# GpSimd's constants written during the decay, rows on ScalarE's queue, second weights right behind the first: one change to an attention-and-MoE kernel

## The chip, the cores and the metric

The kernel runs on one core of a Trainium2 chip. The metric is device time in microseconds (us) of one execution; a kernel is run several times and its median is given with the lowest and the highest run. Profiles come from one execution each, and their span is some 2 us shorter than the time of the run. PE is the matmul engine TensorE, PEld its weight loads, DVE is VectorE, ACT is ScalarE, POOL is GpSimd, SP is SyncE, and a "q" behind a name (SPq, ACTq) is the part of that engine that issues DMAs.

## The reference, cut to what matters

```python
# attention with a decay: q, k, v are (8, 8, 576, 64), f is (8, 8, 576)
scores = scale * np.matmul(q, k.transpose(0, 1, 3, 2))
cum = np.cumsum(np.log(np.clip(f, 0.0001, 1.0)), axis=-1)
scores = np.where(causal, -1e9, scores + cum[:, :, :, None] - cum[:, :, None, :])
attn = softmax(scores)                      # written out in the reference
x = (attn @ v) as (8, 576, 512)
# moe: w_in (512, 1024), a 3-tap convolution along the sequence, w_out (1024, 512)
h = np.maximum(x @ w_in, 0.0)               # "moe1" in this text
conv_out = sum(conv_w[k] * shifted(h, k) for k in range(3))
out = (h * sigmoid(conv_out)) @ w_out       # "moe2"
```

## The kernel before

Heads are worked four at a time: a **half batch** is four heads of one batch, and there are sixteen; two heads are a **pair**. Q and K of a half batch are loaded transposed by SP into a ring of buffers, and the decay enters the scores as extra rows of these buffers: high and low parts of the cumulative sums (`khi`, `klo`), written by small DMAs. VectorE "clamps" those buffers (it turns some rows into constants), the scores are multiplied, ScalarE takes the exponentials, the product with V is normalised ("norm", VectorE), transposed, and when both half batches of a batch are through, moe1 of that batch starts.

The head of the kernel is written out by hand. The rest is a list of tasks with estimated times; a function plays them through once, with a model of each engine and of the DMA traffic, and every engine's instructions are then written in the order in which the play started them. The engines keep that order on the chip, whatever they find there. I call this function **the planner**.

```python
def rows_first(p, eng):                       # the decay's rows of half batch 0
    eng.dma_start(tq[126:127, c], khi4[r, :])
    eng.dma_start(tk[96:97, c], khi4[r, :])
    eng.dma_start(tk[98:99, c], klo4[r, :])
# ... the head, in this order: decay of the first four heads, rows_first(0, nc.scalar),
# decay of all heads, then
rows_first(1, nc.gpsimd)
load_v(0, 0, HH); load_v(0, HH, H)
nc.gpsimd.dma_start(kd[0], khi_sb)            # the decay's copies in DRAM
nc.gpsimd.dma_start(kd[1], klo_sb)
# ... then GpSimd's constants: ones and zeros in va, ident, borders of ht
# ... tasks; keys are priorities, the lowest goes first
WAITS = ((3, 0), (3, 1), (4, 0), (4, 1))      # second weights behind these clamps
for j, (h, side) in enumerate(WAITS):
    if h == hb:
        x = task({"DVE": 0.1}, [even[1] if side == 0 else even[-1]], -9,
                 lambda j=j: hold(w_out_f16[:, 2 * j:2 * j + 2, :]))
        t_wout.append(task({"POOL": 0.8}, [x], 2 * hb - 1.0, lambda j=j: load_w_out(j),
                           lag=2.0, dma=1.7))
```

`hold` is a write of one element by VectorE into the weights' buffer, so that the load behind it can't start earlier.

## Time and profile before

| | before |
|---|---|
| median of 3 runs | 272.54 us (272.22 to 273.33) |
| profiled span, mean PE clock | 271.1 us, 0.976 of full |
| PE, DVE, ACT busy | 241.7, 226.9, 212.1 us |
| PE full (over 9.5 of 10 us) | from about 74 to 235 us |
| PE's holes between 44 and 72 us | 5.1 us |
| first moe1 starts | 38.33 us |

How to read it: PE is the bound for most of the run, so the time is set by how soon PE gets full and stays full. The lines that show this stand in the prediction.

### The profile page before, as it was taken

What the parts mean: (1) busy time and instruction counts of PE and PEld (TensorE: products, weight loads), DVE (VectorE), ACT (ScalarE), POOL (GpSimd) and SP (SyncE); (2) the same over time, 40 slices, a digit from 0 to 9 for tenths busy, and PEclk for the clock granted to TensorE, in tenths of its full rate; (3) what the DMA queues carried; (4) which work ended last, traced back from release to release, by engine and by line L of the source; (5) the groups of instructions that cost most, each with busy time, mean ns of one, the idle gap of its engine ahead of it and who ended that gap; (6) DMA issues with size and microseconds to landing.
All of it is one profiled execution on the core that took longest, in us unless ns stands there. A gap on an engine that the chain in (4) does not pass through costs nothing.

```text
span 271.1 us, 6621 instructions
## 1 busy us (share of the span) xinstructions
PE 241.7 (89%) x2602; PEld 166.1 (61%) x2602; DVE 226.9 (84%) x401; ACT 212.1 (78%) x347; POOL 59.2 (22%) x124
## 2 busy tenths in 40 slices
PE   2864869878899999999999999999999999989990
PEld 1333646646677777776776677667776777655540
DVE  5863538999799999999989989999899999978751
ACT  5081727989879999989989899989889998577552
POOL 4491110631120340332315050406010100000000
PEclk9999868999999999999999999999999999999997
DMA  8999999999998999999999999999101201022015
GB/s 138 202 209 177 223 184 221 222 183 246 168 220 183 219 244 166 228 167 256 269 213 180 203 245 185 223 160 278 61 28 52 80 0 58 23 116 80 0 46 226
DMA packets 121284, 44.58 MB, mean 164 GB/s; under 512 B 115560, under 2 KB 116596, under 8 KB 121254
## 3 DMA queue, kind: packets, MB, share of 16 engines
q1 hardware_dynamic: 115088, 32.00, 66.9%
q0 software_dynamic: 5840, 12.01, 17.0%
q8 instruction: 20, 0.33, 0.5%
q10 hardware_dynamic: 326, 0.17, 0.4%
q14 instruction: 10, 0.08, 0.1%
HBM read 13.99 MB, written 9.58 MB: 87 GB/s over the span
## 4 chain that ended last, share of the span: by engine, by line
PE 64%; DVE 8%; DMA 7%; issue 6%; SPq 6%; ACT 5%; POOL 0%; DVEq 0%; ACTq 0%; POOLq 0%
PE mm L425 19%; PE mm L487 19%; PE sc L298 10%; PE O L356 8%; DMA stk<-in_k_dram 6%; SPq L110 5%; PE sc L330 4%; DVE u L457 2%; PE sc L500 2%; PE mm L393 2%; DVE u L455 2%; SPq L163 1%; ACT ht L438 1%; DMA out_dram<-ob 1%; ACT po L324 1%
## 5 line engine op out<-in xcount | busy, mean ns | idle before, releaser
L425 PE MATMUL mm<-xt,w_in_f 128*128 128x288 f16 x512 | 80.3, 292 | 1.7 <-DVE xt L413 0.4
L298 PE MATMUL sc<-stq,stk 128*128 128x128 bf16 (+3 forms) x576 | 67.3, 242 | 8.1 <-ACT pm L338 3.6
L324 ACT ACTIVATE po<-sc 128x1024 f16<-128x1024 f32 x64 | 64.6, 1028 | 2.6 <-PE sc L298 2.1
L438 ACT ACTIVATE ht<-mm 128x288 f16<-128x288 f32 x128 | 52.0, 414 | 12.3 <-PE mm L425 11.2
L298 PEld LDWEIGHTS <-stk 128*128 128x128 bf16 x576 | 42.4, 99 | 28.7 <-issue 7.7
L425 PEld LDWEIGHTS <-w_in_f 128*128 128x128 f16 x512 | 48.2, 100 | 18.7 <-issue 3.1
L487 PE MATMUL mm<-w_out_f,hg 128*128 128x512 f16 x248 | 58.4, 379 | 0.7 <-ACT xt L411 0.6
L455 DVE SCALAR_TENSOR_TENSOR u<-ht,cwt 128x576 f32<-128x576 f16 x64 | 51.5, 810 | 5.4 <-ACT ht L438 4.7
L457 DVE SCALAR_TENSOR_TENSOR u<-ht,cwt,u 128x576 f32<-128x576 f16 x64 | 51.5, 810 | 0.5
L475 DVE SCALAR_TENSOR_TENSOR hg<-hg,ht 128x576 f16<-128x576 f16 x56 | 41.6, 751 | 4.4 <-ACT hg L467 4.0
L467 ACT ACTIVATE hg<-u,cwt 128x576 f16<-128x576 f32 x56 | 43.4, 780 | 1.0 <-DVE u L457 0.9
L338 ACT ACTIVATE pm<-sc 128x1024 f16<-128x1024 f32 x32 | 32.9, 1028 | 11.8 <-PE sc L298 11.7
L487 PEld LDWEIGHTS <-hg 128*128 128x128 f16 x248 | 23.5, 98 | 24.2 <-issue 0.9
L356 PE MATMUL O<-va,po 128*128 128x65 f16 x640 | 36.6, 194 | 1.2 <-ACT po L324 1.0
L356 PE MATMUL O<-va,pm 128*128 128x65 f16 x256 | 31.1, 194 | 3.0 <-DVE xn L369 1.8
L356 PEld LDWEIGHTS <-po 128*128 128x128 f16 x640 | 30.5, 97 | 2.4 <-ACT po L324 1.8
L356 PEld LDWEIGHTS <-pm 128*128 128x128 f16 x256 | 24.1, 98 | 5.7 <-DVE xn L369 2.7
L369 DVE TENSOR_TENSOR xn<-O,rc 128x640 f16<-128x640 f32 x32 | 26.4, 824 | 1.1
L132 POOL DMA_DIRECT2D stq<-consts x23 | 12.2, 535 | 66.8 <-PE mm L425 27.0
L330 PE MATMUL sc<-trib,identb 128*128 128x512 bf16 x64 | 24.5, 383 | 1.2 <-ACT po L324 1.1
L511 ACT ACTIVATE ob<-mm 128x512 f32<-128x512 f32 x23 | 13.7, 598 | 11.0 <-PE mm L487 10.7
L522 POOL DMA_DIRECT2D out_dram<-ob x10 | 7.7, 768 | 44.2 <-ACT ht L438 21.9
(112 smaller groups left out, 223.8 us busy)
## 6 DMA issues: line engine op xcount, KB each, us to landing
vf<-in_v_dram SPq DMA_DIRECT2D x64, 128.0 KB, 4.0
out_dram<-ob POOLq DMA_DIRECT2D x10, 512.0 KB, 6.4
out_dram<-ob SPq DMA_DIRECT2D x10, 256.0 KB, 2.1
stq<-consts POOLq DMA_DIRECT2D x8, 216.0 KB, 4.7
vf<-in_v_dram SPq DMA_DIRECT2D x16, 64.0 KB, 5.2
w_in_f<-in_moe_w_in_dram POOLq DMA_DIRECT2D x1, 1024.0 KB, 10.7
w_out_f<-in_moe_w_out_dram POOLq DMA_DIRECT2D x4, 256.0 KB, 5.6
out_dram<-ob SPq DMA_DIRECT2D x2, 512.0 KB, 2.8
```

Source lines behind the costliest of these rows:

```text
L298: nc.tensor.matmul(sc, stk_t[hb % RING][:, k0:k0 + 128], stq_t[hb % RING][:, q0:q0 + w], start=start, stop=stop, skip_group_check=True)
L324: nc.scalar.activation(p_of[i, s][:, 0:1024], sc_of.pop((i, s)), AF.Exp, scale=SCALE)
L330: nc.tensor.matmul(sc[:, 512 * s:512 * (s + 1)], identb, trib, start=True, stop=False, skip_group_check=True)
L338: nc.scalar.activation(p_of[i, 2], sc_of.pop((i, 2)), AF.Exp, scale=SCALE)
L356: nc.tensor.matmul(O[:, s, 65 * Q:65 * (Q + 1)], w, va[:, h, m, :], start=(m == 0), stop=(m == Q))
L425: nc.tensor.matmul(ps[:, 0:w], w_in_f16[:, cc, 128 * ff:128 * (ff + 1)], xt[:, cc, w * t:w * (t + 1)], start=(cc == 0), stop=(cc == NCC - 1))
L438: nc.scalar.activation(ht[:, 0, HT_0 + w * t:HT_0 + w * (t + 1)], ps[:, 0:w], AF.Relu)
L455: nc.vector.scalar_tensor_tensor(u, hl, cwt[:, ff, 0:1], hc, op0=ALU.mult, op1=ALU.add)
L457: nc.vector.scalar_tensor_tensor(u, hr, cwt[:, ff, 1:2], u, op0=ALU.mult, op1=ALU.add)
L467: nc.scalar.activation(hv, u, AF.Tanh, scale=cwt[:, ff, 2:3])
L475: nc.vector.scalar_tensor_tensor(hv, hv, 1.0, hc, op0=ALU.add, op1=ALU.mult)
L487: nc.tensor.matmul(ps, chunk(g, ff, c), w_out_f16[:, ff, :], start=(ff == 0), stop=(ff == NFF - 1))
```

## The change

The intent has four parts. GpSimd writes its constants while VectorE prepares the decay, and the second set of rows of half batch 0 is issued by ScalarE, so GpSimd is free for the rows of half batch 1. The copies of the decay to DRAM go behind those rows. The second weights are loaded in one go behind norm 3, right after the first weights and ahead of most of half batch 3. The planner gets other priorities (`AHEAD`: it may run attention four steps ahead instead of three). It also gets three changed estimates of times, which the cut below leaves out. `CLAMPS` and `HALVES` say from which half batch on VectorE no longer clamps Q's buffer and V is loaded in whole batches.

```diff
-    def rows_first(p, eng):
+    def rows_first(p):
-        eng.dma_start(tq[126:127, c], khi4[r, :])
+        nc.scalar.dma_start(tq[126:127, c], khi4[r, :])     # and the two others
 ...  (the loops that write GpSimd's constants move up, ahead of load_qk(1, 0, 4))
-    rows_first(1, nc.gpsimd)
+    rows_first(1)
-    nc.gpsimd.dma_start(kd[0], khi_sb)                      # now a task behind the rows of half batch 1
-    nc.gpsimd.dma_start(kd[1], klo_sb)
-    CLAMPS, HALVES, LANDING = 8, 16, 3.0
+    CLAMPS, HALVES, LANDING = 6, 8, 3.0
-    WAITS = ((3, 0), (3, 1), (4, 0), (4, 1))
+    WAITS = ((3, 2), (3, 2), (3, 2), (3, 2))                # 2: behind norm 3
 ...  (rows of half batch 1 as two tasks, one for Q's row and one for K's)
-    ... 2 * hb - 1.1 + 0.5 * p, ... cast_v
+    ... 2 * hb - 0.6 + 0.5 * p, ... cast_v
-    t_norm[i] = task({"DVE": 1.05}, [t_pv[i, 1]], i - 0.0, ...
+    t_norm[i] = task({"DVE": 1.05}, [t_pv[i, 1]], i - 1.0, ...
 ...  (relu, conv, gate and evac: keys moved likewise)
-    AHEAD, QUEUED = 3.0, 8.0
+    AHEAD, QUEUED = 4.0, 8.0
```

## The prediction

> **What bounds the kernel now.** I read the stretches of four microseconds first, because the shares of the whole span (PE 89%, DVE 84%, ACT 78%) mix stages. The columns are: stretch, its length, busy time of PE, PEld, DVE, ACT and POOL, then the granted PE clock, the DMA share and GB/s.
>
> ```profile
> 20.00:24.00 4.00, 1.24 (x31) 1.04 (x31) 1.05 (x3) 0.00 (x0) 1.45 (x3) 1.00 1.31 134
> 24.00:28.00 4.00, 2.93 (x27) 2.39 (x28) 1.91 (x5) 1.97 (x3) 0.00 (x0) 0.75 1.15 237
> 32.00:36.00 4.00, 1.94 (x43) 1.40 (x39) 2.75 (x7) 1.72 (x2) 0.38 (x1) 1.00 1.25 242
> 36.00:40.00 4.00, 2.60 (x16) 1.73 (x17) 1.22 (x3) 1.43 (x2) 0.64 (x2) 0.53 1.13 154
> 40.00:44.00 4.00, 4.00 (x24) 2.65 (x23) 2.92 (x6) 1.88 (x5) 0.50 (x1) 0.62 1.13 245
> 56.00:60.00 4.00, 2.84 (x27) 1.95 (x27) 4.00 (x9) 3.52 (x8) 0.73 (x1) 1.00 1.27 188
> ```
>
> There are three stages. Up to about 41 us every compute engine has holes while the DMA share stays above 1. From 44 to 72 us DVE is full (4.00 of 4) and PE is not: its busy times there leave 0.3+0.0+1.2+1.2+0.8+0.8+0.8 = 5.1 us. From about 74 to 235 us PE is full; the stretches of twenty microseconds there show 19.6 to 20.0. So nothing in the last stage can shorten the kernel, and what counts is how early PE gets full. PE's holes between 20 and 44 us sum to 2.8+1.1+0.0+2.1+1.4+0.0 = 7.3 us, and two cold stretches come on top (clock 0.75, then 0.53 and 0.62): the 24 moe1 matmuls from 38.33 us take 5.42 us, where eight in the full-clock stage take 0.98 us (24 would take 2.9), a loss of 2.5 us.
>
> Next, the GpSimd timeline and PE's waits, for the thing that the change names.
>
> ```profile
> 10.80 0.70 POOL L125 DMA_DIRECT2D stq<-khi  x1 [6.81 <-DVE stq L119]
> ...
> 13.64 0.31 POOL L262 MEMSET va<- 64x260 f16 x1
> ...
> 18.75 0.92 POOL L140 DMA_DIRECT2D stk<-khi_sb  x1
> ...
> 20.15 0.50 POOL L142 DMA_DIRECT2D stq<-khi_sb  x1
> ```
>
> ```profile
> PE sc L298 <- DMA stq<-khi_sb: 2.7, 1, 2.7
> ```
>
> GpSimd stands idle for 6.81 us before 10.80, then writes constants from 13.64 to 17.57, and only then issues the decay rows of half batch 1, the last of which lands at 25.07, where PE has waited 2.7 us for it.
>
> Last, the chain that ended last, which starts in the loads. Columns: start, length, what.
>
> ```profile
> 10.43 5.89 DMA stk<-in_k_dram
> 16.34 0.73 SPq L163
> ...
> 20.13 4.19 SPq L110
> 24.36 10.71 DMA stk<-in_k_dram
> 35.10 0.88 DVE stk L119
> 36.14 0.84 DVE xn L369
> 37.02 0.61 PE mm L393 x4
> 38.33 5.42 PE mm L425 x24
> ```
>
> The reader is to see that the wait of 2.7 us is not on it. The chain goes through the SP queue: K of half batch 1 lands at 16.3, the rest of V is issued, then Q and K of half batch 2; K lands at 35.1 after 10.7 us beside the first weights. Its clamp on DVE (L119) stands ahead of the norm of pair 3 (L369), although PE had that pair's product ready at 34.9. That norm gates the transpose and the first moe1.
>
> **What the Trainium skill says.** "SBUF — State Buffer", section "Who interferes with whom": GpSimd shares a port pair with VectorE, held for a whole instruction by whichever starts first, in VectorE's two-port modes or against reads of GpSimd. So constants beside VectorE's decay work could slow one of the two. In the trace of before the same memsets ran beside VectorE's 1.02 us memsets of consts, at 0.31 us each; no clash is visible, but the mixture is not the same. "DMA: Bandwidth & Descriptors", section "Latency and other measured facts", gives a longer time to the first byte for GpSimd's DMAs than for those of a hardware queue (about 1 us against 600 ns). The trace agrees in direction: the first rows took 3.2 and 3.6 us from the ACT queue, the second ones 3.8 to 4.0 us from GpSimd. The same page, section "Issuing engines are not separate DMA queues": moving an issue saves the sequencer's time only, the 16 engines are shared. "TensorE: Matmul & The Clock Gate", section "What's actually happening": after an idle window of about 3.4 us PE runs at half clock. The granted 0.53 after the holes at 32 to 38 us agrees.
>
> **The change part by part.**
>
> 1. *Constants earlier.* 13.64 to 17.64 is 4.0 us of GpSimd; they fit in the hole of 6.8 us (3.99 to 10.80). GpSimd then has only DMA issues left. Cost on the path: none, if the port does not bite.
>
> 2. *Rows of half batch 0, second part, on ACT's queue.* Three issues of about 0.55 us from 10.5, the last from 11.6; plus 3.2 us it lands at 14.8, where before PE got it at 15.96. ACT issues until 12.2 and its first exponential starts at 12.92, so ACT loses nothing. Local gain about 1 us, of which V's landing (18.2) hides most.
>
> 3. *Rows of half batch 1.* Q's row can go when Q has landed (15.4), K's rows when K has (16.3). Two rows of K at about 0.55 us and two fills at 0.55 us put the last issue near 17 to 17.5; with the 4.9 us that these rows took, the scores can start at 21.9 instead of 25.07. Local gain 3.2 us, and the cold stretch after the hole (26 to 29 us, half clock) should vanish.
>
> 4. *The decay's copies to DRAM later.* Two of 72 KB leave 12.5 to 13.6 us, where they took 17% of the engines for 3 us, 0.5 us. K of half batch 1 and V come that much sooner, and with them the SP chain: about 0.5 us.
>
> 5. *But parts 2 and 3 meet the chain.* The planner at the end of the kernel writes each engine's order once. Walking it by hand with the new constants, it still assumes K of half batch 2 before norm 3 is ready, so the clamp stays ahead of that norm on DVE. K's landing moves only by part 4, from 35.1 to about 34.6. The 3.2 us are then spent waiting there: moe1 starts about 0.5 us earlier, and again cold. On the path: -0.5 us.
>
> 6. *Second weights behind the first.* Four issues of 0.73 us and 1 MB, moved from 49-60 us to about 34-40 us. It frees GpSimd from waiting on its holds (10.0 us of waits between 36 and 60), but Q, K and V of half batch 3 get some 5 us of traffic ahead of them (first weights: 10.7 us to landing while sharing). Before, K of half batch 3 landed at 43.2 and was clamped only at 50.5, so there are 7 us of room. Second weights were first used at 76.8, which waited for the last gate of batch 0 (68.6), not for weights. On the path: 0.
>
> 7. *Priorities.* Attention may run 4 instead of 3 steps ahead, norms come earlier, gates later. One step of attention is about 2.8 us of PE by the full-clock rows and about 2.5 us of DVE; one unit of moe1 is 0.98 us of PE for 2.4 us of DVE (two of 0.81 and one of 0.75). More attention in the stage where DVE is full puts more PE work against the same DVE work, so part of the 5.1 us fills. I choose 2 us: -2.0 us.
>
> 8. *Two half batches fewer clamped on DVE.* Two clamps of 0.87 us, 1.7 us of DVE, at about 80 to 100 us where PE is full: 0. V in whole batches from batch 4 on: 0.
>
> Sum: -0.5 - 2.0 = -2.5 us. I add -0.6 us for one chance in seven that norm 3 gets ahead of that clamp and moe1 starts some 4 to 5 us sooner. 272.5 - 3.1 = 269.4 us.
>
> **The rivals.**
>
> (a) *The head's gain comes through whole.* Norm 3 is not held, PE goes from half batch 1 into moe1 at 33 us without a cold clock. For it: the first weights land near 31.6, and PE's holes and cold loss of 20 to 44 us (7.3 + 2.5 + about 1.5) are large enough. Against: the chain shows K's landing, not the rows. It would give -5 to -7 us for the head, with part 7 about 264 to 266 us.
>
> (b) *All is swallowed.* K of half batch 2 holds norm 3, priorities give nothing since ACT is at 3.5 to 3.8 of 4 in the middle stage as well. It would give 272 us.
>
> (c) *The second weights delay half batch 3 and VectorE stalls in order on its clamp.* For it: the DMA share is above 1 there and the queue's holes are short. Against: 7 us of room. It would cost 1 to 3 us, 272 to 274 us with the rest.
>
> (d) *GpSimd's constants slow VectorE's decay.* The cumulative sums and clamps (0.18 to 1.34 us each) would slip by at most one GpSimd instruction each, 0.1 to 0.9 us; the first scores, now at 12.06, would come up to 1 us later.
>
> **Range and chances.** Between (a) at 265 and (b) at 272, with the middle at 269.4, I set 266.6 to 271.9. Faster by over 2% needs less than 267.1 us, which takes (a) or a far larger part 7: 0.2. Slower by over 2% needs (c) and (d) far beyond their sizes: 0.02. The rest, 0.78, is within 2%.
>
> **What would show it.** Part 1 and 3: GpSimd's constants end before 9 us, the rows of half batch 1 are issued by 18 us, the first scores of that half batch start near 22 us and the clock stays at 1.0 until 30 us. Part 5: the chain still has K of half batch 2 landing near 34.6, its clamp, then norm 3; moe1 starts near 37.8 with a clock near 0.5. Part 7: PE's holes from 44 to 72 us shrink from 5.1 to about 3 us. If moe1 starts before 35 us, step 5 is wrong and (a) holds. If a clamp of half batch 3 waits for a DMA on DVE, (c) holds. If the first scores start after 12.6 us, (d) holds.

## The result, and the profile after

| | before | after |
|---|---|---|
| median | 272.5 us (272.22 to 273.33, 4 runs) | 276.58 us (276.01 to 277.23, 4 runs) |
| ratio | 1 | 1.0145, interval 1.0111 to 1.0179 |
| profiled span, mean PE clock | 271.1 us, 0.976 | 275.5 us, 0.954 |
| PE's holes between 44 and 72 us | 5.1 us | 6.0 us |
| first moe1 starts | 38.33 us | 40.52 us |

The change made the kernel some 4 us slower; predicted were 3.1 us in the other direction. Ratios, here and below, are the mean time of one kernel's fast runs over that of the other's from the same rounds, so they aren't quite the ratio of the medians. "Fast" leaves out runs that the records mark as slow, over 1.5% above the fastest of the same kernel.

The stretches of four microseconds after the change, columns as in the prediction (stretch, length, PE, PEld, DVE, ACT, POOL, PE clock, DMA share, GB/s):

```profile
20.00:24.00 4.00, 3.31 (x21) 1.79 (x20) 0.02 (x1) 2.14 (x4) 0.00 (x0) 0.50 1.14 229
24.00:28.00 4.00, 2.57 (x48) 1.97 (x47) 1.42 (x5) 2.71 (x3) 0.05 (x1) 0.87 1.01 199
32.00:36.00 4.00, 3.55 (x56) 2.68 (x55) 2.47 (x11) 3.15 (x4) 0.00 (x0) 1.00 1.11 192
36.00:40.00 4.00, 2.14 (x42) 1.75 (x42) 1.94 (x7) 0.83 (x2) 0.54 (x1) 0.83 1.28 190
40.00:44.00 4.00, 3.62 (x18) 2.34 (x16) 1.14 (x3) 2.09 (x4) 3.39 (x6) 0.50 1.24 178
64.00:68.00 4.00, 2.06 (x40) 1.47 (x37) 3.96 (x7) 4.00 (x6) 0.78 (x1) 1.00 1.21 147
68.00:72.00 4.00, 2.05 (x28) 1.54 (x29) 3.97 (x10) 1.01 (x2) 2.49 (x4) 0.68 1.00 204
72.00:76.00 4.00, 4.00 (x22) 2.54 (x21) 3.60 (x6) 2.15 (x6) 0.00 (x0) 0.50 1.24 199
```

The same three last stretches of the kernel before:

```profile
64.00:68.00 4.00, 3.23 (x53) 2.30 (x52) 3.93 (x7) 3.58 (x6) 0.00 (x0) 1.00 1.30 244
68.00:72.00 4.00, 3.18 (x47) 2.54 (x47) 3.54 (x5) 3.22 (x5) 1.23 (x2) 1.00 1.01 200
72.00:76.00 4.00, 3.93 (x59) 3.14 (x57) 2.46 (x4) 3.91 (x8) 0.79 (x2) 1.00 1.15 166
```

Two things are new. In the head the clock is at 0.50 from 20 to 24 us, where before it was at 1.00. And from 64 to 72 us PE has only 2.06 and 2.05 us of work, after which its clock falls to 0.50: the 22 matmuls from 72 to 76 us, in part of other shapes, fill the same four microseconds as 59 did before. Up to 72 us PE had done 66 matmuls of moe1 and 144 of the scores, before 70 and 172. From 80 us on PE is full in both kernels, so the 4 us were lost before that.

First the head. GpSimd (start, length, then what ended the idle time before):

```profile
4.03 0.51 POOL L238 MEMSET va<- 64x260 f16 x1
...
7.21 0.11 POOL L245 MEMSET ht<- 128x4 f16 x1
...
15.32 1.10 POOL L141 DMA_DIRECT2D stk<-khi_sb  x1 [0.28 <-DMA stk<-in_k_dram]
```

The constants lie where they were meant to lie, and the rows of half batch 1 are issued at 15.32 where before it was 18.75. ScalarE, in the same profile:

```profile
18.14 0.47 ACTq L127 DMA_DIRECT2D stk<-klo  x1
18.66 1.02 ACT L338 ACTIVATE pm<-sc 128x1024 f16<-128x1024 f32 x1 [12.36 <-DMA stk<-khi]
```

ScalarE stands idle for 12.36 us before its first exponential at 18.66, which came at 12.92 before. It's held by its own three row DMAs, issued at 15.12, 16.19 and 18.14, where GpSimd had issued them at 10.80, 11.49 and 12.03 before. The waits in the compiled program say why (this list is not from the profile):

```
ACT: L125 rows of stq  waits DMAHW0 and DVE     owner so far: K of half batch 1 (SP)
ACT: L126 rows of stk  waits DMAHW3 and DVE     owner so far: V, first DMA (SP)
ACT: L127 rows of stk  waits DMAHW6             owner so far: V, third DMA (SP)
```

All DMAs of SP and ACT share eight completion semaphores, DMAHW0 to DMAHW7, handed out in turn by the framework that builds the program. The row DMAs got those of K of half batch 1 and of two loads of V, and each first waits until that load has landed. The trace bears this out: by its semaphore records the three loads landed at 15.04, 16.11 and 18.12, and the three issues follow within 0.1 us of them. On GpSimd's queue the same DMAs waited for VectorE alone.

Next the chain that ended last (start, length, what):

```profile
22.71 4.87 DMA stk<-in_k_dram
...
35.09 0.78 DVE stk L119
...
36.03 0.83 DVE xn L369
...
38.32 0.82 DVE xn L369
...
40.52 4.00 PE mm L425 x16
```

The clamp of half batch 2's keys (L119) stands on DVE ahead of norm 2 (L369) now; before it stood ahead of norm 3 only. But here it took its 0.8 us and waited for no load: K of half batch 2 had landed at 27.6. The first weights, which wait for norm 0 and so for ScalarE, were issued only then:

```profile
27.95 0.86 POOL L640 DMA_DIRECT2D w_in_f<-in_moe_w_in_dram  x1 [9.12 <-DVE w_in_f L153]
```

Before, they were issued at 21.41, K loaded beside them and landed at 35.1. So ScalarE's stall makes the norms late and, by the way, K early. moe1 starts 2.2 us later and at half clock: 16 matmuls take 4.00 us (before, too, it was cold: 24 in 5.42), where eight take 0.98 us at full clock.

Last the middle. The second weights are issued early, as intended, and PE's own line (start, length) of the hole reads:

```profile
39.46 2.89 POOL L157 DMA_DIRECT2D w_out_f<-in_moe_w_out_dram  x4 [8.61 <-DVE w_out_f L153]
```

```profile
70.41 0.61 PE L393 MATMUL mm<-ident,xn 128*128 128x128 f16 x4 [1.45 <-DVE xn L369]
...
71.72 4.00 PE L425 MATMUL mm<-xt,w_in_f 128*128 128x288 f16 x16 [0.38 <-DVE xt L413]
```

PE waits for the last norms of batch 1, transposes, waits again and goes into moe1 cold. It has nothing else to do there, because of the order that the planner wrote. PE's order around that point in the three kernels that matter (tasks with their count of matmuls; from the compiled programs, not the profile):

```
before           transposes 8+4, value product 15, scores of half batch 4 ..., moe1 8
                 (the first scores of half batch 4 stand ahead of the transposes)
after            transposes 8+4, moe1 16, and only then the scores of half batch 4
after, second    scores of half batch 4, transposes 8+4, scores of half batch 4, ..., moe1 8
weights as before
```

### The profile page after: what moved, and what is told of

The parts are those of the page before. It is cut to its first block, busy times and chain, and to the rows that moved or that the text cites. A ratio compares the mean times of both kernels' runs of the same rounds, so it can differ in the third digit from the quotient of the medians.

```text
span 275.5 us, 6580 instructions
## 1 busy us (share of the span) xinstructions
PE 243.4 (88%) x2602; PEld 167.4 (61%) x2602; DVE 227.5 (83%) x404; ACT 209.6 (76%) x342; POOL 60.7 (22%) x123
## 4 chain that ended last, share of the span: by engine, by line
PE 72%; DVE 8%; ACT 7%; SPq 6%; DMA 3%; issue 2%; ACTq 0%; DVEq 0%
PE mm L425 21%; PE mm L487 19%; PE sc L298 12%; PE O L356 9%; SPq L110 5%; PE sc L330 4%; ACT po L324 2%; PE sc L500 2%; PE mm L393 2%; DMA stk<-in_k_dram 2%; DVE xn L369 1%; DMA vf<-in_v_dram 1%; ACT ht L438 1%; DVE u L455 1%; DVE hg L475 1%
## 5 line engine op out<-in xcount | busy, mean ns | idle before, releaser
L425 PE MATMUL mm<-xt,w_in_f 128*128 128x288 f16 x512 | 81.3, 296 | 2.5 <-DVE xt L413 0.8
L298 PE MATMUL sc<-stq,stk 128*128 128x128 bf16 (+3 forms) x576 | 68.3, 245 | 9.5 <-ACT pm L338 6.0
L324 ACT ACTIVATE po<-sc 128x1024 f16<-128x1024 f32 x64 | 65.3, 1028 | 2.1 <-PE sc L298 1.5
L298 PEld LDWEIGHTS <-stk 128*128 128x128 bf16 x576 | 43.2, 100 | 31.3 <-issue 11.3
L425 PEld LDWEIGHTS <-w_in_f 128*128 128x128 f16 x512 | 48.8, 100 | 19.4 <-issue 4.0
L438 ACT ACTIVATE ht<-mm 128x288 f16<-128x288 f32 x128 | 51.1, 413 | 11.1 <-PE mm L425 10.4
L132 POOL DMA_DIRECT2D stq<-consts x25 | 15.0, 602 | 79.5 <-DMA stq<-in_q_dram 33.5
L369 DVE TENSOR_TENSOR xn<-O,rc 128x640 f16<-128x640 f32 x32 | 26.4, 824 | 1.1
L330 PE MATMUL sc<-trib,identb 128*128 128x512 bf16 x64 | 25.1, 392 | 1.1 <-ACT po L324 1.1
L367 DVE RECIPROCAL rc<-O 128x10 f32<-128x10 f32 x32 | 6.9, 217 | 14.2 <-PE O L356 14.1
L511 ACT ACTIVATE ob<-mm 128x512 f32<-128x512 f32 x19 | 11.4, 598 | 9.4 <-PE mm L487 9.2
```

The lines of the kernel that those rows point to most:

```text
L298: nc.tensor.matmul(sc, stk_t[hb % RING][:, k0:k0 + 128], stq_t[hb % RING][:, q0:q0 + w], start=start, stop=stop, skip_group_check=True)
L324: nc.scalar.activation(p_of[i, s][:, 0:1024], sc_of.pop((i, s)), AF.Exp, scale=SCALE)
L330: nc.tensor.matmul(sc[:, 512 * s:512 * (s + 1)], identb, trib, start=True, stop=False, skip_group_check=True)
L425: nc.tensor.matmul(ps[:, 0:w], w_in_f16[:, cc, 128 * ff:128 * (ff + 1)], xt[:, cc, w * t:w * (t + 1)], start=(cc == 0), stop=(cc == NCC - 1))
L438: nc.scalar.activation(ht[:, 0, HT_0 + w * t:HT_0 + w * (t + 1)], ps[:, 0:w], AF.Relu)
```

## The experiments

Eighteen kernels were run; all gave correct results. Each is named by its label. "Changed" means the changed kernel. In eleven of them the edit makes the planner write a new order of work; the text says where the order was kept.

### The rows on ScalarE's queue: b_rowsact and a_rowspool

The kernel before with the rows on ScalarE's queue, and the changed kernel with them back on GpSimd's.

```diff
 b_rowsact                                   a_rowspool
-    rows_first(1, nc.gpsimd)               -    rows_first(1)
+    rows_first(1, nc.scalar)               +    rows_first(1, nc.gpsimd)
```

> The kernel before, with one edit: the same three rows issued from ACT instead of GpSimd. Theory L: ACT's first exponential moves from 12.9 to about 18.7 us, PE's first products of probabilities and V from 18.7 to about 25 us, and the time rises by 2 to 6 us, to 274.5 to 278.5 us. Rival M or P: the head and the time stay within 1 us of 272.5.

> The changed kernel, with the three decay rows of half batch 0's second part issued from GpSimd again instead of from ACT; the order of all engines otherwise the same. Theory L (the three rows on ACT's queue share eight completion semaphores with the SP queue; each waits until K of half batch 1, V1 and V3 have landed, and ACT stands behind them until 18.7 us): the rows are issued by 12.6 us, ACT's first exponential starts near 13 us instead of 18.66, norm 0 ends near 21 us instead of 27.6, moe1 starts 2 to 5 us sooner than 40.5 us, and the time falls by 4 to 8 us to 269 to 272.5 us. Rival M (the new priorities in the middle stage cost the time): the head moves as above but the end moves by less than 2 us, 275 us or more. Rival P (GpSimd's constants beside VectorE's decay work slowed the head): ACT's first exponential stays after 16 us.

b_rowsact: 277.55 us (273.83 to 280.61) beside 272.27; half of its six runs are slow, and the fast ones give 1.0102 (1.0056 to 1.0148), about 2.8 us. Alone, the stall and what follows from it cost that much; with so many runs left out as slow this is the low figure (the medians of all runs differ by 5.3 us). a_rowspool: 276.85 us, 1.0164 (1.0129 to 1.0199): no gain, against my expectation, although its head is mended: the scores of half batch 1 start at 21.86 and PE doesn't wait for the rows. Its DVE timeline shows what holds it instead:

```profile
35.19 0.88 DVE L119 TENSOR_SCALAR stk<-stk,lim 96x2304 uint16<-96x2304 uint16 x1 [3.74 <-DMA stk<-in_k_dram]
...
36.22 0.82 DVE L369 TENSOR_TENSOR xn<-O,rc 128x640 f16<-128x640 f32 x1
```

DVE stands idle for 3.74 us until K of half batch 2 lands, because that clamp is next in its order, with norm 2 behind it. PE has 1.45 us of work from 32 to 36 us, and moe1 starts at 41.09. So moe1 comes at about the same time by two different ways. With the stall, the norms are late and K is early; without it, the first weights are issued at 21.15, K lands beside them at 35.2, and the clamp makes the norms wait.

### The priorities: a_oldkeys, a_rowspool_oldkeys, b_newkeys

The changed kernel with the seven old priorities and the old look-ahead, the same with the rows on GpSimd, and the kernel before with the new ones.

```diff
-    AHEAD, QUEUED = 4.0, 8.0        # a_oldkeys; b_newkeys is the reverse
+    AHEAD, QUEUED = 3.0, 8.0        # and the keys of cast, norm, relu, conv, gate, evac
```

> The changed kernel with the eight old priorities and the old look-ahead of 3 steps; the head is as in the changed kernel, rows on ACT. Theory L: ACT's first exponential still at about 18.7 us, the time within 1.5 us of 276.6. Rival M: the time falls by 2.5 us or more to 274 us or less, and PE's second cold stretch at 68 to 76 us is gone.

> Both edits: rows from GpSimd and old priorities. If L and M are independent the fall is the sum of the falls of the two single edits, within 1 us. Theory L alone: the same time as the version with only the rows moved back, within 1 us.

> The kernel before with the new planner priorities and the larger look-ahead alone. If the new priorities gain what they gained in the changed kernel (279.7 to 276.7): 269 to 270.5, 2 to 3 us faster, which is also what the prediction's step 7 says (2.0). Rival (they only repair what the early second weights break): 271.5 to 273.

a_oldkeys: 279.69 us beside 272.27, 1.0268 (1.0219 to 1.0317). a_rowspool_oldkeys: 279.55 us, 1.0261 (1.0225 to 1.0297). Neither of my theories had expected a rise. So in the changed kernel the new priorities save about 3 us, and they aren't the cause of the loss. b_newkeys: 273.73 us beside 272.54, 1.0048 (1.0013 to 1.0083), where 269 to 270.5 was expected. Alone they cost a little. Their worth depends on what they meet: they repair something that the rest of the change breaks.

### The second weights, planned anew: a_rowspool_oldwaits, a_oldwaits, b_newwaits

The changed kernel with the second weights back at their old places (with the rows on GpSimd, and with the rows left on ScalarE), and the kernel before with its second weights behind norm 3 and nothing else.

```diff
-    WAITS = ((3, 2), (3, 2), (3, 2), (3, 2))     # a_oldwaits; b_newwaits is the reverse
+    WAITS = ((3, 0), (3, 1), (4, 0), (4, 1))
```

> Rows from GpSimd, and the second weights loaded at the four places of the kernel before. Theory W: the Q, K and V loads of half batch 4 start 4 to 6 us sooner (K before 49 us instead of 52), its scores stand ahead of the transposes of batch 1 on PE, PE's holes of 3.6 us in 64 to 72 us and the cold stretch after them go, and the time falls by 2.5 to 5 us to 272 to 274 us, though moe1 still starts at about 41 us. Rival C: less than 1.5 us.

> The changed kernel with only the load of the second weights put back behind norms and clamps of half batches 3 and 4 (the head keeps the rows on ScalarE's queue). Theory W (the early second weights are the main cost): the ones with rows on GpSimd and old places measured 274.6 against 276.85 with early places, so here 274.0 to 275.0, 1.5 to 2.5 us below the changed kernel, the matmul-engine hole from 64 to 72 us gone (busy over 3 of 4 us in both windows). Theory L (ScalarE's stall at the head costs, once the second loss is taken out): 1 to 3 us above the kernel with rows on GpSimd and old places, so 275.6 to 277.6, with the first moe1 stage still near 40.5 us.

> The kernel before with one part of the change alone: all four loads of the second weights issued behind norm 3. Theory W: 274.5 to 278, that is 2 to 5 us slower, with queries of half batch 4 issued 2 us or more later than in the kernel before (44.4 us) and a hole in the matmul engine between 64 and 76 us with its clock at 0.5 to 0.7 there. Rival (step 6 of the prediction, path cost 0, the loss is due to the other parts together): 271.8 to 272.8.

a_rowspool_oldwaits: 274.6 us (271.57 to 275.15) beside 271.72, 1.0111 (1.0096 to 1.0125). a_oldwaits: 272.97 us beside 272.54, 1.0019 (0.9976 to 1.0063): with this one line taken back, the whole loss is gone, though ScalarE's stall is still in it and moe1 starts at 40.1, 1.8 us later than in the kernel before. Both of my theories had expected a longer time. Its stretch from 68 to 72 us:

```profile
68.00:72.00 4.00, 3.74 (x53) 2.82 (x52) 3.73 (x7) 4.00 (x6) 1.04 (x2) 1.00 1.02 190
```

b_newwaits: 281.6 us (280.11 to 283.23), 1.0346 (1.0308 to 1.0384), 9 us slower and far beyond what I expected. The early second weights are the main cost. But each of these three kernels was planned anew, so the order of work changed with the load.

### The second weights with the order kept: b_early_fixed, a_late_fixed

Here the play's order stays exactly as it was in the parent kernel, on every engine. The weights' tasks remain in the plan as empty ones, and only the moment at which the loads and their holds are written moves: in the kernel before to norm 3, in the changed kernel to the old places.

```diff
             fn()
+        if number == t_norm[3]:                      # b_early_fixed
+            for j in range(4):
+                hold(w_out_f16[:, 2 * j:2 * j + 2, :])
+                load_w_out(j)
+        if number in places:                         # a_late_fixed; places are the old clamps
+            j = places.index(number)
+            hold(w_out_f16[:, 2 * j:2 * j + 2, :])
+            load_w_out(j)
```

> The kernel before with its own order of work on every engine kept instruction for instruction; only the four loads of the second weights, and the small writes that hold them back, are issued right behind norm 3 (near 38 us) instead of at 49 to 60 us. Theory W1 (the cost is the traffic: Q, K and V of half batches 3 and 4 load beside the second weights and land later): 274.5 to 278, at least 2 us slower, K of half batch 3 taking over 5 us to issue instead of 2.8. Theory W2 (the cost of the early load, 9.4 us slower when planned, is the planner's other order of work): 271.8 to 273.2, the same as before.

> The changed kernel with its own order on every engine kept; only the loads of the second weights and their holds are issued behind the clamps of half batches 3 and 4, as in the kernel before. Theory W1 (traffic): 273 to 275, i.e. 2 to 4 us faster than the changed kernel, near the planned version with old places (272.97). Theory W2 (order): 276 to 277, no gain, the hole at 64 to 76 us with its low clock still there.

b_early_fixed: 275.35 us (274.74 to 277.44) beside 272.23, 1.013 (1.0095 to 1.0166): the traffic alone costs about 3 us in the order of before. The issues on SP's queue (start, length), one link of the chain and one clamp show it; the profiled run is the slowest of the five, so they may show somewhat too much:

```profile
37.60 6.69 SPq L110 DMA_TRANSPOSE stk<-in_k_dram  x1
44.34 6.49 SPq L163 DMA_DIRECT2D vf<-in_v_dram  x5
50.94 4.32 SPq L110 DMA_TRANSPOSE stq<-in_q_dram  x1
```

```profile
48.55 6.45 DMA vf<-in_v_dram
```

```profile
51.77 0.88 DVE L119 TENSOR_SCALAR stk<-stk,lim 96x2304 uint16<-96x2304 uint16 x1 [2.64 <-DMA stk<-in_k_dram]
```

In the kernel before, the same three issues (K and V of half batch 3, Q of half batch 4) were:

```profile
38.41 2.84 SPq L110 DMA_TRANSPOSE stk<-in_k_dram  x1
41.30 3.03 SPq L163 DMA_DIRECT2D vf<-in_v_dram  x5
44.44 2.46 SPq L110 DMA_TRANSPOSE stq<-in_q_dram  x1
```

Beside the 1 MB of weights K takes 6.69 us to issue instead of 2.84, V 6.49 instead of 3.03, and Q of half batch 4 begins 6.5 us later. K of half batch 3 lands at about 51.7, 8.5 us later than before (43.2), and its clamp on DVE waits for it. V of half batch 3 lands at 55.0, and PE is busy for 1.59 and 1.79 us in the stretches from 52 and 56 us, where before it was 2.79 and 2.84.

a_late_fixed: 275.89 us beside 272.23, 1.0134 (1.01 to 1.0168), the same as the changed kernel's 1.0145. Loading late doesn't help in the changed kernel's order. Its hole is still there:

```profile
68.00:72.00 4.00, 2.36 (x18) 1.48 (x16) 3.97 (x9) 1.55 (x2) 3.05 (x6) 0.56 1.26 251
```

So of the changed kernel's loss, what a_oldwaits takes back (1.0145 to 1.0019) is the planned order, not the traffic. In b_newwaits the traffic by itself is worth 1.3 of the 3.5%, if it costs there what it cost in the old order; the other 2.2 would come with the new order. No run tests that sum. Its PE order has the same pattern at batch 1, 24 moe1 matmuls right behind the transposes.

### Later still: a_later

```diff
-    WAITS = ((3, 2), (3, 2), (3, 2), (3, 2))
+    WAITS = ((4, 0), (4, 0), (4, 1), (4, 1))
```

> An attempt to beat both: the changed kernel with the second weights later than in the kernel before, all behind the clamps of half batch 4. If the traffic beside half batches 3 and 4 is what costs (W1): 270.5 to 272.5, under the 272.97 of the version with the old places. If it's the planner's order (W2): anything from 271 to 276, without a relation to when the loads are issued.

276.89 us, 1.0197 (1.0155 to 1.0239). Later traffic didn't help; this too was planned anew. Its PE order doesn't have the pattern at batch 1, so that pattern isn't the only way to lose.

### The head without the rest: b_constsearly, a_rowspool_oldall

b_constsearly is the kernel before with GpSimd's constants moved up, all orders kept. a_rowspool_oldall is the changed kernel with the rows on GpSimd, and the old priorities, places of the second weights, `CLAMPS` and `HALVES`; what is left of the change is the head's order and the planner's three estimates.

```diff
+    (loops of GpSimd's constants)                # b_constsearly
     load_qk(1, 0, 4)
```

> The kernel before with only GpSimd's constants written ahead of VectorE's decay, all orders otherwise kept. The prediction's step 1 (no cost): 272.0 to 273.0. Rival d of the prediction (GpSimd's writes slow VectorE's decay): VectorE's clamp of the first keys 0.9 us instead of 0.58 and the first scores about 0.5 us later; at the end up to 1 us, 273 to 273.6.

> The kernel before with only the order of the head changed: GpSimd's constants before the decay, the rows of half batch 1 as a separate query row and key rows, the copies of the decay behind them, rows of the second quarter on GpSimd's queue as before; second weights, priorities and the planner's thresholds as before. If the head order is worth what the prediction's steps 1, 3 and 5 say: 271.5 to 272.5 (half a us). Rival (the clamp of the third half batch's keys now stands ahead of norm 2, moe1 begins near 41 us instead of 38.3): 273.5 to 276.

b_constsearly: 272.28 us beside 272.23, 1.0016 (0.9983 to 1.0048). No cost, and the clamps of the first half batch took 0.57 to 0.58 us as before. a_rowspool_oldall: 276.31 us beside 272.54, 1.0147 (1.0123 to 1.0172). That is the rival's result: the clamp of half batch 2's keys stands ahead of norm 2 (34.62, then 35.66 us), PE's busy time from 32 to 36 us is 0.00, and moe1 starts at 40.86. That the late moe1 is what costs isn't shown: this kernel was planned anew, and a_oldwaits starts moe1 almost as late (40.1) without a loss.

### The clamp moved by the planner: a_rowspool_cl3, a_cl3, a_rowspool_cl3_oldwaits

In these the planner is told that the clamp of half batch 2's keys comes after norm 3.

```diff
-    even.append(task({"DVE": 0.9}, [x], ...
+    even.append(task({"DVE": 0.9}, [x] + ([t_norm[3]] if (hb, s) == (2, 1) else []), ...
```

> Rows from GpSimd, and the clamp of half batch 2's K made to follow norm 3 in the planner, so it no longer stands ahead of norms 2 and 3 on VectorE. Theory C (with the rows mended, that clamp, which waits for K's landing at 35.2 us, takes the place of the lost time): norm 2 ends near 29 to 32 us instead of 37, moe1 starts at 33 to 36 us instead of 41.1, and the time falls by 3 to 6 us from 276.85, to 271 to 274 us. Rival W (the second weights' early load costs the time, in the middle stage): moe1 starts earlier, but the hole at 64 to 72 us stays and the time falls by less than 2 us.

> The changed kernel with rows still on ACT, only that clamp put after norm 3. Theory L plus C (either of the two alone holds moe1 near 40.5 us, so that each hides the other): moe1 starts at most 1.5 us sooner than 40.5 us and the time stays within 1.5 us of 276.6; the gain of the same edit with the rows on GpSimd is at least 2 us larger. If L plays no part: the same gain as there.

> Rows from GpSimd, the clamp after norm 3, the second weights at the old places. If C and W add: the falls of the two single edits summed, within 1.5 us, which would be 267 to 271 us, below the kernel before. If the middle stage is bound by the same thing either way: no better than the better of the two.

a_rowspool_cl3: 280.88 us beside 271.72, 1.0307 (1.0278 to 1.0336). moe1 came early (PE busy 3.93 of 4 us from 36 to 40 at full clock), but PE then had 0.41 us of work from 52 to 56: K of half batch 3 took 8.35 us to issue beside the second weights. a_cl3: 280.9 us, 1.0303 (1.0255 to 1.0351); its profile fell in a slow run (314.85 us) and is not used. a_rowspool_cl3_oldwaits: 275.48 us, 1.0119 (1.0081 to 1.0156). With the second weights at their old places the loss is far smaller, but the version isn't better than a_rowspool_oldwaits. The first two rose where I had expected a fall and no change. Again every one had been planned anew.

### The clamp moved by hand: b_clampmoved, a_rowspool_oldwaits_clampmoved

One instruction moves, the clamp of half batch 2's keys, to right behind norm 3 in the finished order; everything else is kept.

```diff
     order, est = play()
+    numbers = [k for k, _ in order]
+    at = numbers.index(t_load["clamp"])
+    late = order.pop(at); numbers.pop(at)
+    order.insert(numbers.index(t_norm[3]) + 1, late)
```

> The kernel before, its order kept on every engine, but on VectorE the one clamp of the third half batch's keys stands behind norm 3 instead of ahead of it. By the prediction's step 5 that clamp (35.10 to 35.98) is the link between the keys' landing and moe1's start at 38.33. Theory S (a start of moe1 that comes sooner reaches the end, as steps 5 and 7 of the prediction assumed): moe1 0.8 to 1.2 us earlier, near 37.3, and the whole 271.0 to 271.8, some 0.8 us faster. Rival (the pipeline's later order swallows it): moe1 earlier but the time within 0.3 us of before, 272.0 to 272.6.

> An attempt to beat both: the changed kernel with the rows back on GpSimd's queue, the second weights back at their old places and the same clamp moved behind norm 3 on VectorE, all other orders kept. Theory S: moe1 near 37 us instead of 39 to 41, and the time 271.5 to 273, below the 274.6 of the version without the move. Rival: 274 to 275, unchanged.

b_clampmoved: 271.94 us beside 272.09, 0.9985 (0.9948 to 1.0023). moe1 did start earlier, by 1.7 us, though 1.0 us of this was there at norm 2 already (32.09 for 33.06), ahead of the moved clamp:

```profile
34.40 0.82 DVE L369 TENSOR_TENSOR xn<-O,rc 128x640 f16<-128x640 f32 x1
35.14 0.87 DVE L119 TENSOR_SCALAR stk<-stk,lim 96x2304 uint16<-96x2304 uint16 x1
```

```profile
36.59 3.80 PE mm L425 x20
```

The time doesn't show it. Between 48 and 68 us PE was busy for 13.5 us, in the kernel before for 16.1: the lead was given back there. a_rowspool_oldwaits_clampmoved: 270.76 us (269.88 to 276.16) beside 272.09, 0.994 (0.9911 to 0.9969), where its parent a_rowspool_oldwaits had 1.0111. In that order the one moved instruction is worth 1.7%, over 4 us by the ratios (the two were run in different rounds). It's the fastest kernel, 0.6% ahead of the kernel before and 2% ahead of the changed one. Its profile fell in its one slow run, so I don't read it further. Its parent had one fast run among six, 271.57 us, which is the profiled one: there K of half batch 2 landed before 31.4, the clamp hardly waited, and norm 2 began at 32.40. One run is a hint only, but it points to the same lock.

## Why the prediction was wrong

The prediction said 269.4 us (266.6 to 271.9); measured were 276.58. Within 2%, which it had given most of the chances, was right; the direction and the range weren't.

**Step 6, "On the path: 0", failed, and it's the main error.** I compared one landing (K of half batch 3) with one clamp, found 7 us of room and put some 5 us of traffic against it. In the order of before, K came 8.5 us later and the clamp waited 2.64 us (b_early_fixed). Two things were left out besides. The load stands ahead of V of half batch 3 and of everything of half batch 4 as well: b_early_fixed measured about 3 us for all this traffic. And the planner counts the traffic and writes another order of work: a_oldwaits against a_late_fixed shows that in the changed kernel the order is what costs, from 1.0019 to 1.0134, about 3 us. Rival (c) named the traffic and sized the total at 272 to 274 us. Its sign, a clamp of half batch 3 that waits for a DMA, came in b_early_fixed and not in the changed kernel, where that clamp (51.92) waited for none. It was right about which part would cost, but in the changed kernel the way was another one.

**Step 2, "ACT loses nothing", failed.** ScalarE lost 5.7 us (first exponential at 18.66 instead of 12.92), because its row DMAs wait for completion semaphores that loads of SP still hold. I had read only the time of the issues. Alone it costs about 2.8 us (b_rowsact, fast runs). In the changed kernel it costs nothing that can be seen (a_rowspool): without it, K of half batch 2 lands at 35.2 instead of 27.6, and the clamp holds moe1 to about the same time.

**Step 3** was right for the rows themselves: issued by 17 us, and with the rows on GpSimd the scores start at 21.86, predicted 21.9. That match is partly luck: K's rows had landed by 20.0 (semaphore records), and PE came to the scores straight from other work. In the changed kernel they started at 28.65, by step 2, and the clock, which was to stay at 1.0, was at 0.50 from 16 to 24 us. **Step 4** fits: Q of half batch 2 was issued at 19.74 instead of 20.13, predicted 0.5 us. **Step 1** was right: b_constsearly is within the noise. Rival (d) met its own sign, but not its cost. The first scores start at 13.03 in the changed kernel and at 13.48 in b_constsearly, both past the 12.6 us that I had set, and one clamp took 0.96 us in the changed kernel, 0.58 before. But in b_constsearly the clamps are as short as before and the scores wait 1.84 us for a row's landing, and in a_oldwaits, with the same constants, they start at 11.69. So this scatters by a microsecond and doesn't reach the end.

**Step 5** failed in the changed kernel. It had K of half batch 2 land near 34.6, hold norm 3 by its clamp and let moe1 start near 37.8. K landed at 27.6 and held nothing; moe1 started at 40.52, by the trace because ScalarE, and so the norms, were late. Its lock is there once the stall is gone, and larger than it said: with the new head and estimates the planner put the clamp ahead of norm 2 too, where it waits 3.74 us for K in a_rowspool and 3.90 in a_rowspool_oldall. a_rowspool_oldwaits_clampmoved shows the clamp's part by itself: over 4 us in that order. In b_clampmoved a start of moe1 that was 1.7 us earlier gave nothing that could be resolved, so a gain at the head doesn't simply add to the end, as the sum assumed.

**Step 7, "-2.0 us", failed as a number that stands alone.** In the kernel before, the priorities cost 0.5%; in the changed kernel they save 1.2%. PE's holes from 44 to 72 us were predicted to shrink to 3 us; they grew to 6.0 us.

**Step 8** wasn't tested by itself. The 0.6 us for a lucky order had its sign wrong in the end: I treated the planner's order as a small chance in one place, and it was the largest term.

Three readings of the prediction were loose: from 44 to 72 us DVE was busy for 26.5 of 28 us, not full throughout; ACT had 3.1 to 4.0 of 4 there, not 3.5 to 3.8; and the DMA share was 0.86 from 16 to 20 us. And in the kernel before, PE was not idle for 3.4 us ahead of the half clock that the prediction took as agreeing: the clock fell at 36.2, and PE's longest pause in the 4 us before that was 1.35 us.

What stays open: which part of the new order costs. The kernels with the early load that I compared (changed, b_newwaits, a_oldkeys) all put moe1 of batch 1 ahead of the scores of half batch 4, and the profile of the changed kernel shows PE's hole and its cold clock there. But I didn't move that block by hand, and a_later lost without the pattern. So the pattern is the likely cause, not a shown one. A rival stands beside it: all eleven kernels that were planned anew came out between 1.0019 and 1.0346 of the kernel before, whatever the edit. The old order may just be a good one, and a new order a draw that costs 0 to 3.5%; I didn't measure how far orders scatter by themselves. Also not settled is why a_oldwaits, with ScalarE's stall in it, was not slower than a_rowspool_oldwaits, which has the same order on every engine but for the rows' queue. The traces offer a reason: in a_oldwaits K of half batch 2 was in at 26.7, before the first weights were issued (27.86), and the clamp at 34.90 waited for nothing.

## What to carry to other kernels

When a planner writes the order of work, a moved load is two changes, its traffic and a new order. Keep the order and move the load alone before you say what the load costs, since here the same load cost 1.3% in one kept order, nothing that could be seen in another, and 3.5% with a new order. Before a DMA goes to another engine's queue, look up which completion semaphore it will reuse, because an in-order engine waits for the earlier owner. And look in the order of an engine for a task that waits for a load ahead of one that is ready; moving one such instruction was the best gain in one order, and nothing that could be seen in another.

## What the Trainium skill lacked or had wrong

- "DMA: Bandwidth & Descriptors", section "Issuing engines are not separate DMA queues", weighs another issuing engine by the sequencer time that it saves. It lacks there that the issue may have to wait, and the new engine's compute with it (that such a wait is the issuing sequencer's stands elsewhere on the page): ScalarE stood idle for 12.36 us behind three DMAs of 2.2 KB, whose completion semaphores SP's loads still held. The same page's section "Rules for kernel authors" says to dedicate one semaphore to a DMA; this program shares eight among all DMAs of SP and ACT, and the price in time of sharing is not there: about 2.8 us of 272 (b_rowsact, fast runs).
- "TensorE: Matmul & The Clock Gate", section "What's actually happening", gives an idle window of about 3.4 us for the fall to half clock. In the changed kernel the clock fell to 0.50 between 69 and 70 us, although PE's longest gap until then was 1.39 us; PE had been busy for 1.9 of the 4 us from 65 to 69 us. So a stretch that is half idle in pieces was enough. Another section of the page tells of a kernel where short pauses did the same, but how much activity keeps the clock up is in neither.
- "SBUF — State Buffer", section "Who interferes with whom", led to rival (d). With GpSimd's constants beside VectorE's decay the second clamp took 0.80 to 0.96 us in five of fourteen profiles (0.96 in the changed kernel, 0.80 in a_late_fixed) and 0.57 to 0.62 in the other nine; in the six kernels with the constants later it took 0.58 each time. So the clash, if it is that, comes and goes. The page says that the later one is blocked, but has no measured size for this mix. The time shows no cost: the ratio of b_constsearly is 1.0016 (0.9983 to 1.0048).
